# Output matmuls of one head alternate with score matmuls of a later head

## The chip, the cores and the metric

The kernel runs on one core of one Trainium2 chip. The metric is the device time in microseconds of one execution; the time before is the median of three runs. The engines are named as the profile does: PE is TensorE, with PEld for its weight loads (they overlap the matmuls), DVE is VectorE, ACT is ScalarE, POOL is GpSimd, and SP is the engine that issues most of the DMAs.

## The reference

Attention with two kinds of masks, and behind it a feed-forward layer on the attention's output. Batch 8, 8 heads, 576 positions, head size 64; heads 0 to 3 are local (each position sees the last 32), heads 4 to 7 strided (each position sees those at a distance of a multiple of 32). The feed-forward layer has 4608 tokens, 512 in, 2048 hidden.

```python
    pos = np.arange(S)
    rel = pos[:, None] - pos[None, :]
    mask_local = (rel >= 0) & (rel < stride)
    mask_strided = (rel >= 0) & (pos[None, :] % stride == pos[:, None] % stride)
...
    scores = np.where(masks[None, :, :, :], scores, -1000000000.0)
    scores = scores - np.max(scores, axis=-1, keepdims=True)
    attn = np.exp(scores)
    attn = attn / (np.sum(attn, axis=-1, keepdims=True) + 1e-09)
    return np.matmul(attn, v).astype(np.float32)
...
    h = np.maximum(x @ w_in, 0.0)
    return (h * h @ w_out).astype(np.float32)
```

## The kernel before

The tokens are cut into 12 chunks of 384. Each chunk has 16 slots of 128 hidden columns. For a slot, `up` (line 483) makes the hidden tile `h` from the chunk's `x` with 12 matmuls of 384 columns, ACT and DVE square it and split it into a high part `gh` and a low part `gl`, and `down` (line 512) adds it to the chunk's output `y` with 9 matmuls of 512 columns. Full precision comes from high and low halves: `x`, the weights, `q`, `k`, `v` and the probabilities are all split, the high half rounded by ACT (a cast), the low half the difference, mostly by POOL (`tensor_sub`).

While chunk c goes through the feed-forward layer, the attention for chunk c+1 is made. The strided heads are made on POOL, DVE and ACT alone (`strided`, line 414), and end with the tiles `xsh` (ACT) and `xsl` (POOL, line 476). The local heads need PE. For chunks 0 and 1 `pe_pair` makes them, two at a time. From chunk 2 on `pe_head` (line 208) makes one head in six steps, each a stretch of a Python generator up to its `yield`: load `qk` and `v`; cast (`kx` and `qx`, high halves on ACT, low halves on POOL in lines 229 and 231); score (four matmuls of 256 moving columns and 96 stationary ones, two to a bank, in line 248, with the mask added and the minimum taken by DVE); soft (exponentials and scaling on ACT); turn (`vx`, transposes on DVE, the probabilities split into `px` with a copy in a PSUM bank, lines 267 to 283); and output (four matmuls of 192 moving and 128 stationary columns, line 294, a copy by ACT and two additions by DVE to each bank of two). There are 40 such heads, four to a chunk.

PE's order is written out by hand. From slot 16 on the main loop (line 683) takes two slots at a time: two `up`, then two `down` of the slots before. The lists `plans` (line 603) say which heads go a step further: ahead of `up`, between `up` and `down`, and behind `down`. The first list is for chunk 1, the second for later chunks; they differ in where the first two heads are scored: between `up` and `down` in the first, ahead of `up` in the second. An instruction traced in `tc.issue_after(i)` stays behind `i` in the queue of `i`'s engine; it orders one engine only and is no wait. What isn't tied so is ordered by the compiler.

Three ties matter below. The last weight splits (POOL, line 180) are put behind `last["xs"]`, the strided `xsl` of chunk 1 (line 713). The steps for chunk 2's heads are put behind the last weight step of each engine (`weights_end`, line 615). And head 0 of chunk 2 is loaded and cast at slot 14 (line 724).

Of the kernel before, what the change touches and what calls it, by code (L numbers as in the profile page):

```python
# [7 lines left out]
F32 = mybir.dt.float32  # L8
# [79 lines left out]
def attn_moe(ctx: ExitStack, tc, qk_l, v_l, qk_d, v_d, qk_p, v_p, f_s, q_s, k_s, v_s, w_in, w_out, masks, eye, out):  # L88
# [117 lines left out]
    staged = {}  # L206

    def pe_head(c, h):
        u = f"{c}_{h}"

        def bank(nm):
            return psum(3 + next(turn) % 2, f"{nm}{u}")

        def buf(pl, nm, n, tag, **kw):
            return pl.tile([P, n], F32, name=f"{nm}{u}", tag=tag, **kw)

        qk, vp = buf(lraw, "qk", TC + KC, "qk"), buf(lraw, "v", NW * D, "v")
        qr, kr = qk[:, :TC], qk[:, TC:]
        vr = vp.rearrange("p (w d) -> p w d", d=D)
        kw, wins = KW, [(at, 0 if qc == 0 else 1) for _, qc, at in windows(c)]  # L220
        nk = wins[-1][0] + KW
        nc.sync.dma_start(out=qk[:, : TC + nk], in_=qk_l[c, h, :, : TC + nk])
        last["s"] = nc.sync.dma_start(out=vp, in_=v_l[c, h])
        yield

        qx = lpool.tile([P, TC], F32R, name=f"qx{u}", tag="qh", bufs=1)
        kx = lpool.tile([P, 2, KC], F32R, name=f"kx{u}", tag="kx", bufs=1)
        nc.scalar.copy(kx[:, 0, :nk], kr[:, :nk])
        nc.gpsimd.tensor_sub(kx[:, 1, :nk], kr[:, :nk], f32(kx[:, 0, :nk]))
        nc.scalar.copy(qx, qr)  # L230
        nc.gpsimd.tensor_sub(qx[D:], qr[D:], f32(qx[D:]))
        yield
        e = buf(lpool, "e", 512, "e")
        if h % 2 == 0:
            staged[c] = e
        nmax = small.tile([P, 2 * NW], F32, name=f"nm{u}", tag="nm")
        ssum = sums[h % 3]
        rs = small.tile([P, 2 * NW], F32, name=f"rs{u}", tag="rs")[:, :NW]
        cut = lambda w: slice(w * kw, (w + 1) * kw)
        reduce = lambda w, src, m: nc.vector.tensor_tensor_reduce(  # L240
            out=e[:QC, cut(w)], in0=src, in1=m, scale=-SCALE, scalar=3.0e38,
            op0=ALU.add, op1=ALU.min, accum_out=nmax[:QC, w : w + 1],
        )
        for a in range(0, NW, 2):
            s_ps = bank(f"s{a}")
            for w in (a, a + 1):
                k0 = wins[w][0]
                last["mm"] = nc.tensor.matmul(s_ps[:QC, 256 * (w - a) : 256 * (w - a + 1)], qx[:, w * QC : (w + 1) * QC], kx[:, :, k0 : k0 + kw], start=True, stop=True)  # L248
            sv = s_ps[:QC].rearrange("p (w t k) -> p w t k", w=2, t=2)
            m = wins[a][1]  # L250
            ev = e[:QC, a * kw : (a + 2) * kw].rearrange("p (w k) -> p w k", w=2)
            nc.vector.tensor_add(ev, sv[:, :, 1, :], mask_sb[:QC, m : m + 2, :])
            for w in (a, a + 1):
                reduce(w, sv[:, w - a, 0, :], e[:QC, cut(w)])
        yield
        for w in range(NW):
            nc.scalar.activation(e[:QC, cut(w)], e[:QC, cut(w)], AF.Exp, bias=nmax[:QC, w : w + 1], scale=-1.0, accum_out=ssum[:QC, w, :1])  # L257
        nc.vector.tensor_reduce(out=rs[:QC], in_=ssum[:QC, :NW], op=ALU.add, axis=AX.X)
        nc.vector.reciprocal(rs[:QC], rs[:QC])
        if h != HL - 1:  # L260
            for w in range(NW):
                nc.scalar.mul(e[:QC, cut(w)], e[:QC, cut(w)], rs[:QC, w : w + 1])  # L262
        else:
            ew = e[:QC, : NW * kw].rearrange("p (w k) -> p w k", k=kw)
            last["g"] = nc.gpsimd.tensor_mul(ew, ew, rs[:QC].unsqueeze(2).broadcast_to([QC, NW, kw]))
        yield
        vx = lpool.tile([P, NW, 2, D], F32R, name=f"vx{u}", tag="vx", bufs=1)
        nc.scalar.copy(vx[:, :, 0, :], vr)
        nc.gpsimd.tensor_sub(vx[:, :, 1, :], vr, f32(vx[:, :, 0, :]))
        pt = p_t[h % 2]  # L270
        for r in range(QC // STR):
            for k in (r, r + 1):
                nc.vector.transpose(  # L273
                    out=pt[STR * k : STR * (k + 1), :, STR * r : STR * (r + 1)],
                    in_=e.rearrange("p (w k) -> p w k", k=KW)[STR * r : STR * (r + 1), :, STR * k : STR * (k + 1)],
                )
        src = pt.rearrange("p w q -> p (w q)")
        px = lpool.tile([P, 2, TC], F32R, name=f"px{u}", tag="px")

        o_ps = bank("o0")  # L280
        nc.scalar.copy(o_ps[:, :TC], src)
        nc.scalar.copy(px[:, 0, :], src)
        nc.vector.tensor_sub(px[:, 1, :], o_ps[:, :TC], f32(px[:, 0, :]))
        yield
        x = x_tiles(c)
        par, hp = D * (h % 2), h // 2

        src = staged[c][par : par + D, :TC]
        for a in range(0, NW, 2):
            if a:  # L290
                o_ps = bank(f"o{a}")
            for w in (a, a + 1):
                sl = slice(w * QC, (w + 1) * QC)
                last["mm"] = nc.tensor.matmul(o_ps[:, 2 * QC * (w - a) : 2 * QC * (w - a + 1)], vx[:, w].rearrange("p t d -> p (t d)"), px[:, :, sl], start=True, stop=True)  # L294
            ov = o_ps[:, : 4 * QC].rearrange("p (w t q) -> p w t q", w=2, t=2)
            part = src[:, a * QC : (a + 2) * QC].rearrange("p (w q) -> p w q", w=2)
            nc.scalar.copy(part, ov[D:, :, 0, :])
            nc.vector.tensor_add(part, ov[:D, :, 1, :], part)
            nc.vector.tensor_add(part, ov[:D, :, 0, :], part)
        if par:  # L300
            src = staged[c][:, :TC]
            dst = [x["l", s][:, hp, :] for s in "hl"]
            last["a"] = nc.scalar.copy(dst[0], src)
            last["g"] = nc.gpsimd.tensor_sub(dst[1], src, f32(dst[0]))
        yield


    def pe_pair(c, pr, local, qk, vr, es, pt, banks, sm, single):
# [68 lines left out]
        p4 = pt.rearrange("p (h w q) -> p h w q", h=2, w=NW)  # L377
        for h in range(2):
            t = s_ps[h] if s_ps else banks()

            for w in [*range(NW)] * (2 if c == 0 and local and not pr and h else 1):
                nc.tensor.transpose(t[:kw, w * QC : (w + 1) * QC], e4[h][:, w], ident[:QC, :QC])
            if c == 0 and not local:
                nc.vector.tensor_copy(pt[:kw, h * TC : (h + 1) * TC], t[:kw, :TC])
            else:
                last["a"] = nc.scalar.copy(pt[:kw, h * TC : (h + 1) * TC], t[:kw, :TC])
        yield
        x = x_tiles(c)
        if local:
            o = s_ps[0] if s_ps else banks()  # L390

            for w in [*range(NW)] * (3 if c == 0 and not pr else 1):
                for h in range(2):
                    nc.tensor.matmul(o[D * h : D * (h + 1), w * QC : (w + 1) * QC], v4[:kw, h, w], p4[:kw, h, w], start=True, stop=True)
            outs = [(o[:, :TC], [x["l", s][:, pr, :] for s in "hl"])]
        else:
# [3 lines left out]
            for a in range(2):  # L400
                o = s_ps[a]
                for w in range(NW):
                    for h in range(2):
                        p0 = r0 + STR * h
                        nc.tensor.matmul(o[p0 : p0 + STR, w * QC : (w + 1) * QC], v4[:kw, h, w, STR * a : STR * (a + 1)], p4[:kw, h, w], start=True, stop=True)  # L405
# [163 lines left out]
    def pair_at(c, pr, local, place, psum_at):  # L569
        u = f"{c}_{pr}_{int(local)}"  # L570
        buf = lambda pl, nm, n, tag, **kw: pl.tile([P, n], F32, name=f"{nm}{u}", tag=tag, **kw)
        ee = lambda pl, tag: [buf(pl, f"e{h}", 512, tag) for h in range(2)]
        if place == 0:
            b = buf(lraw, "qk", TC + KC, "qk"), buf(lpool, "v", 512, "vx", bufs=1), ee(lpool, "e"), buf(lpool, "pt", 2 * TC, "px")
        elif place == 1:
            b = buf(lraw, "qk", TC + KC, "qk"), buf(ypool, "v", 512, "ysb"), ee(ypool, "ysb"), buf(lpool, "pt", 2 * TC, "px")
        elif place == 2:
            e = buf(xpool, "e", 2 * TC, "xlh")
            b = buf(xpool, "qk", 2 * TC, "xll"), buf(xpool, "v", 2 * TC, "xsl")[:, :512], [e[:, :TC], e[:, TC:]], buf(lpool, "pt", 2 * KC, "kx", bufs=1)[:, : 2 * TC]
        else:  # L580

            t = buf(wpool, "w", 2048, "w7")
            b = buf(xpool, "qk", 2 * TC, "xsh"), buf(spool, "v", 512, "s3", bufs=5), [t[:, :512], t[:, 512:1024]], t[:, 1024 : 1024 + 2 * TC]
# [10 lines left out]
    def local(c):  # L594
# [7 lines left out]
    heads = {}  # L602
    plans = (
        (("", "0", "01"), ("", "1", "012"), ("", "0", "123"), ("", "1", ""), ("2", "", "23"), ("3", "", "23"), ("", "2", "301"), ("", "3", "0")),
        (("0", "", "01"), ("1", "", "012"), ("", "0", "123"), ("", "1", ""), ("2", "", "23"), ("3", "", "23"), ("", "2", "301"), ("", "3", "0")),
    )

    def take(c, which):
# [213 lines left out]
```

## Time and profile before

| what | value |
| --- | --- |
| median of three runs | 873.07 us (872.31 to 874.12) |
| span of the profiled execution | 872.06 us (872.1 on the page) |
| instructions | 14656, of these 4773 matmuls |
| PE busy | 865.1 us |
| DVE, ACT, POOL busy | 640.3, 557.6, 650.6 us |
| mean granted clock of PE | 0.999 |
| output matmuls of `pe_head` (line 294) | 160, 23.4 us busy |
| score matmuls of `pe_head` (line 248) | 160, 25.4 us busy |

The profiled execution has no time of its own beside its span; the runs' median lies 1.0 us above the span. Busy times are unions, and matmuls overlap each other in the records (the end of one is modelled), so the pace of PE is read from the starts of its matmuls. "Granted clock" is the share of full speed that the chip allows PE: 1.00 is 2.4 GHz, 0.50 is 1.2 GHz.

### The profile page before, as it was taken

What the parts mean: (1) busy time and instruction counts of PE and PEld (TensorE: products, weight loads), DVE (VectorE), ACT (ScalarE), POOL (GpSimd) and SP (SyncE); (2) the same over time, 40 slices, a digit from 0 to 9 for tenths busy, and PEclk for the clock granted to TensorE, in tenths of its full rate; (3) what the DMA queues carried; (4) which work ended last, traced back from release to release, by engine and by line L of the source; (5) the groups of instructions that cost most, each with busy time, mean ns of one, the idle gap of its engine ahead of it and who ended that gap; (6) DMA issues with size and microseconds to landing.
All of it is one profiled execution on the core that took longest, in us unless ns stands there. A gap on an engine that the chain in (4) does not pass through costs nothing.

```text
span 872.1 us, 14656 instructions
## 1 busy us (share of the span) xinstructions
PE 865.1 (99%) x4773; PEld 788.0 (90%) x4773; DVE 640.3 (73%) x1902; ACT 557.6 (64%) x1479; POOL 650.6 (75%) x705
## 2 busy tenths in 40 slices
PE   8999999999999999999999999999999999999998
PEld 7888899999999999999999898999898989899997
DVE  5987688788787787877778778778788878762111
ACT  6989766667576576666666656747657566564332
POOL 3798878868887888788879978997998997850000
PEclk9999999999999999999999999999999999999999
DMA  9962521323123032113113202312212021000001
GB/s 354 365 233 82 184 84 46 95 82 109 40 76 104 26 112 84 38 68 104 39 32 98 80 13 75 104 32 75 77 53 80 14 71 61 8 1 1 37 1 37
DMA packets 26940, 71.39 MB, mean 82 GB/s; under 512 B 2992, under 2 KB 9008, under 8 KB 25328
## 3 DMA queue, kind: packets, MB, share of 16 engines
q1 hardware_dynamic: 26432, 70.00, 23.9%
q8 instruction: 37, 0.61, 0.3%
q10 hardware_dynamic: 432, 0.46, 0.2%
q14 instruction: 39, 0.32, 0.1%
HBM read 61.01 MB, written 9.44 MB: 81 GB/s over the span
## 4 chain that ended last, share of the span: by engine, by line
PE 93%; ACT 2%; POOL 2%; DVE 1%; issue 1%; DMA 1%; ACTq 0%; POOLq 0%
PE h L495 44%; PE y L532 44%; PE s L248 2%; PE o L294 2%; ACT b L366 1%; DMA raw<-w_out 1%; PE b L338 1%; POOL w L180 1%; PE w_ps L634 1%; PE b L405 0%; POOL pq L441 0%; DVE raw L170 0%; DVE sums L370 0%; ACT w L176 0%; ACT z L167 0%
## 5 line engine op out<-in xcount | busy, mean ns | idle before, releaser
L532 PE MATMUL y<-w,gh 128*128 128x512 f32 x1152 | 371.4, 391 | 0.4 <-ACT gh L507 0.4
L532 PEld LDWEIGHTS y<-w,gh 128*128 128x128 f32 x1152 | 215.9, 188 | 43.2 <-ACT gh L507 0.8
L464 POOL TENSOR_TENSOR pp<-vs,sc 128x448 f32<-128x448 f32 (+10 forms) x192 | 189.7, 1015 | 49.5 <-DVE qs L465 25.9
L495 PE MATMUL h<-xsh,w 128*128 128x384 f32 x768 | 226.2, 335 | 0.0
L532 PE MATMUL y<-w,gl 128*128 128x512 f32 x576 | 222.6, 390 | 0.0
L495 PE MATMUL h<-xlh,w 128*128 128x384 f32 x768 | 220.5, 337 | 0.0
L441 POOL TENSOR_TENSOR pq<-ks,qs 128x512 f32<-128x512 f32 (+2 forms) x192 | 197.8, 1050 | 24.6 <-DVE sc L442 23.0
L507 ACT CAST gh<-h 128x384 fp32r<-128x384 f32 x192 | 91.7, 477 | 105.0 <-PE y L532 102.7
L505 ACT ACTIVATE h<-h 128x384 f32<-128x384 f32 x176 | 82.6, 471 | 118.5 <-PE h L495 115.9
L508 DVE TENSOR_TENSOR gl<-h,gh 128x384 fp32r<-128x384 f32 x192 | 105.4, 549 | 69.0 <-ACT gh L507 68.0
L442 DVE TENSOR_REDUCE sc<-pq 128x8 f32<-128x512 f32 (+4 forms) x228 | 118.8, 534 | 48.3 <-POOL pq L441 45.3
L495 PEld LDWEIGHTS h<-xlh,w 128*128 128x128 f32 x768 | 140.4, 188 | 2.9
L495 PEld LDWEIGHTS h<-xsh,w 128*128 128x128 f32 x768 | 141.4, 188 | 0.5 <-POOL w L180 0.2
L495 PE MATMUL h<-xsl,w 128*128 128x384 f32 x384 | 128.4, 334 | 0.0
L465 DVE TENSOR_REDUCE qs<-pp 128x64 f32<-128x448 f32 (+11 forms) x192 | 107.2, 563 | 28.2 <-POOL pp L464 26.4
L495 PE MATMUL h<-xll,w 128*128 128x384 f32 x384 | 125.8, 336 | 0.0
L532 PEld LDWEIGHTS y<-w,gl 128*128 128x128 f32 x576 | 108.2, 188 | 19.4
L273 DVE STREAM_TRANSPOSE p_t<-e 32x128 f32<-32x128 f32 x240 | 72.4, 302 | 18.3 <-ACT e L262 13.0
L506 ACT ACTIVATE h<-h 128x384 f32<-128x384 f32 x176 | 82.9, 473 | 3.8
L257 ACT ACTIVATE e<-e,nm 96x128 f32<-96x128 f32 x160 | 62.5, 392 | 19.5 <-DVE nm L240 19.3
L495 PEld LDWEIGHTS h<-xll,w 128*128 128x128 f32 x384 | 71.8, 188 | 2.3
L495 PEld LDWEIGHTS h<-xsl,w 128*128 128x128 f32 x384 | 72.1, 188 | 0.1
(112 smaller groups left out, 1040.9 us busy)
## 6 DMA issues: line engine op xcount, KB each, us to landing
qk<-qk_l SPq DMA_DIRECT2D x24, 400.0 KB, 3.1
y<-ysb SPq DMA_DIRECT2D x35, 256.0 KB, 2.0
raw<-w_in SPq DMA_DIRECT2D x7, 1024.0 KB, 11.1
qk<-qk_l SPq DMA_DIRECT2D x16, 416.0 KB, 3.2
vs<-v_s SPq DMA_DIRECT2D x10, 576.0 KB, 3.8
raw<-w_out SPq DMA_DIRECT2D x5, 1024.0 KB, 12.9
v<-v_l SPq DMA_DIRECT2D x40, 128.0 KB, 2.1
ks<-k_s SPq DMA_DIRECT2D x8, 576.0 KB, 3.8
```

Of the source, the lines that this page charges most:

```text
L257: nc.scalar.activation(e[:QC, cut(w)], e[:QC, cut(w)], AF.Exp, bias=nmax[:QC, w : w + 1], scale=-1.0, accum_out=ssum[:QC, w, :1])
L273: nc.vector.transpose(out=pt[STR * k : STR * (k + 1), :, STR * r : STR * (r + 1)], in_=e.rearrange("p (w k) -> p w k", k=KW)[STR * r : STR ...
L441: nc.gpsimd.tensor_mul(pv, kt[:, a : a + m, :], qt[:, i - i0 : i - i0 + 1, :].broadcast_to([P, m, D]))
L442: nc.vector.tensor_reduce(out=sc[:, i - i0, a : a + m], in_=pv, op=ALU.add, axis=AX.X)
L464: nc.gpsimd.tensor_mul(pv, vt[:, a : a + nd, :n], sc[:, il : il + 1, :n].broadcast_to([P, nd, n]))
L465: nc.vector.tensor_reduce(out=ot[:, il, a : a + nd], in_=pv, op=ALU.add, axis=AX.X)
L495: done = nc.tensor.matmul(ph[:, :TC], wi[p][w][:, wsl], x["ls"[kt // 2], s][:, kt % 2, :], start=n == 0, stop=n == 11)
L505: nc.scalar.activation(g, g, AF.Relu)
L506: nc.scalar.activation(g, g, AF.Square)
L507: last["gh"] = nc.scalar.copy(gh, g)
L508: nc.vector.tensor_sub(gl, g, f32(gh))
L532: done = nc.tensor.matmul(into, g[:, t * P : (t + 1) * P], wo[p][w][:, wsl], start=j == fresh and k == 0, stop=j == NFT - 1 and k == 2)
```

## The change

`pe_head` becomes a class `Head` with the steps `load`, `cast`, `scores`, `soft`, `turn` and `outputs`. `scores(a)` and `outputs(a)` are now half heads: the two matmuls of one bank, returned as a list, and the work on that bank as a function. `visit(o, s)` takes half a head's outputs and half a head's scores of a later head, issues their matmuls in turn (output, score, output, score), each tied behind the one before, and then the work on both banks. All `visit`s stand on PE's queue where `plan` puts them: for each two slots g it gives steps ahead of `up`, two lists between `up` and `down`, and steps behind `down`. In the steady part (g from 14) there is one visit ahead of `up`, with the outputs of half v - 3 and the scores of half v, where v = g - 5; the first six g have their own lists. The outputs go to bank 4, the scores to bank 3.

Around it: outputs are gathered in a tile of their own (`st`) instead of the head's `e`; `px` has one buffer instead of two, `v` three instead of two; the probabilities of `pe_pair` are two tiles, one to each head, and its second place takes the buffers `st` and `qh`.

```diff
+    def chain(make):
+
+        with tc.issue_after(last["pe"].ins):
+            last["pe"] = make()
...
+        def scores(self, a, bank):
...
+            s = psum(bank, f"s{a}{self.u}")
+
+            def product(w):
+                q, k = self.qx[:, w * QC : (w + 1) * QC], self.kx[:, :, self.at[w] : self.at[w] + KW]
+                return nc.tensor.matmul(s[:QC, 256 * (w - a) : 256 * (w - a + 1)], q, k, start=True, stop=True)
...
+            return [lambda w=w: product(w) for w in (a, a + 1)], rest
...
+        def turn(self, bank):
+            self.vx = vx = lpool.tile([P, NW, 2, D], F32R, name=f"vx{self.u}", tag="vx", bufs=1)
...
+            self.px = px = lpool.tile([P, 2, TC], F32R, name=f"px{self.u}", tag="px", bufs=1)
+            copy = psum(bank, f"p{self.u}")[:, :TC]
+            nc.scalar.copy(copy, src)
+            nc.scalar.copy(px[:, 0, :], src)
+            nc.vector.tensor_sub(px[:, 1, :], copy, f32(px[:, 0, :]))
...
+    def visit(o=None, s=None, banks=(4, 3)):
+
+
+        jobs = [heads[n // 2].outputs(2 * (n % 2), banks[0]) for n in ([] if o is None else [o])]
+        jobs += [heads[n // 2].scores(2 * (n % 2), banks[1]) for n in ([] if s is None else [s])]
+        for two in zip(*(products for products, _ in jobs)):
+            for make in two:
+                chain(make)
+        behind_pe(*(rest for _, rest in jobs))
+
+    def behind_pe(*steps):
+        with tc.issue_after(last["pe"].ins):
+            for step in steps:
+                step()
...
-    plans = (
-        (("", "0", "01"), ("", "1", "012"), ("", "0", "123"), ("", "1", ""), ("2", "", "23"), ("3", "", "23"), ("", "2", "301"), ("", "3", "0")),
-        (("0", "", "01"), ("1", "", "012"), ("", "0", "123"), ("", "1", ""), ("2", "", "23"), ("3", "", "23"), ("", "2", "301"), ("", "3", "0")),
-    )
...
+    def plan(g):
+
+
+        n = len(heads)
+        head = lambda k, what: [(what, k)] if 0 <= k < n else []
+        t = g - 8
+        if t == 0:
+            return [("s", 0), ("S", 1)], [("cast", 1), ("soft", 0)], [], [("load", 2)]
+        if t == 1:
+            return [("s", 2), ("S", 3)], [("cast", 2), ("turn", 0)], [], [("soft", 1), ("load", 3)]
+        if t == 2:
+            return [("v", 0, 4)], [], [("v", 1, 5)], [("turn", 1), ("cast", 3), ("soft", 2)]
+        if t == 3:
+            return [("v", 2, None)], [], [("v", 3, None)], [("turn", 2), ("load", 4)]
+        if t == 4:
+            return [("s", 6), ("S", 7)], [("cast", 4), ("soft", 3)], [("v", 4, None)], [("load", 5)]
+        if t == 5:
+            return [("v", 5, 8)], [("turn", 3)], [], []
+        v = g - 5
+        k = v // 2
+        o = v - 3 if 0 <= v - 3 < 2 * n else None
+        s = v if v < 2 * n else None
+        visits = [("v", o, s)] if o is not None or s is not None else []
+        if v % 2:
+            return visits, head(k + 1, "cast") + head(k, "soft"), [], []
+        return visits, head(k - 1, "turn"), [], head(k + 1, "load")
+
+    def do(steps):
+        for what, *k in steps:
+            if what == "s":
+                visit(None, k[0])
+            elif what == "S":
+                visit(None, k[0], banks=(4, 4))
+            elif what == "v":
+                visit(*k)
+            else:
+                h = heads[k[0]]
+                step = getattr(h, what)
+                args = (4,) if what == "turn" else ()
                 with ExitStack() as st:
...
+                    for i in weights_end.values() if h.c == NPLAIN else ():
                         st.enter_context(tc.issue_after(i.ins))
...
+                    behind_pe(lambda: step(*args))
...
-            before, between, rest = plans[c >= NPLAIN][j // 2]
-            for part, slots, two in (up, (s, s + 1), before), (down, (s - 2, s - 1), between):
-                take(c + 1, two)
+            before, middle, between, rest = plan(s // 2)
+            for part, slots, then in (up, (s, s + 1), [before]), (down, (s - 2, s - 1), [middle, between]):
+                for steps in then:
+                    do(steps)
...
-            take(c + 1, rest.strip("01") if j >= NFT - 4 else rest)
-            if j >= NFT - 4:
-                take(c + 2, rest.strip("23"))
+            do(rest)
...
-            take(2, "010")
+            do([("load", 0), ("load", 1), ("cast", 0)])
```

## Rows read from the trace of the kernel before

**Rows 1.** The page's busy times by engine (share of the span, instructions), and its row of PE's granted clock in 40 slices of the span, in tenths.

```profile
PE 865.1 (99%) x4773; PEld 788.0 (90%) x4773; DVE 640.3 (73%) x1902; ACT 557.6 (64%) x1479; POOL 650.6 (75%) x705
...
PEclk9999999999999999999999999999999999999999
```

**Rows 2.** The page's chain of work that ended last, shares of the span by engine.

```profile
PE 93%; ACT 2%; POOL 2%; DVE 1%; issue 1%; DMA 1%; ACTq 0%; POOLq 0%
```

**Rows 3.** Who PE waited for, over the whole span: us in total, times, the longest. Six rows in all, of which the first two and the last are shown; the others are 0.5, 0.4 and 0.3 us.

```profile
PE w_ps L634 <- POOL sums L121: 1.6, 1, 1.6
PE b L382 <- DVE e L375: 0.5, 1, 0.5
...
PE b L382 <- POOL e L375: 0.2, 1, 0.2
```

**Rows 4.** Groups of PE's weight loads by line and shape, whole span: count, then busy us and the mean ns of one, then idle time ahead of them and what ended it.

```profile
L294 PEld LDWEIGHTS o<-px,vx 128*128 128x128 f32 x160 | 23.5, 189 | 0.0
L248 PEld LDWEIGHTS s<-kx,qx 128*96 128x96 f32 x160 | 22.2, 162 | 4.7 <-POOL qx L231 0.5
```

**Rows 5.** Timeline of PE around one visit of output matmuls (start us, duration us, instruction). The second and third line of the four output matmuls come from narrower windows, which leave out the first one and the first two of them.

```profile
303.65 0.34 PE L495 MATMUL h<-xsh,w 128*128 128x384 f32 x1
303.83 0.59 PE L294 MATMUL o<-px,vx 128*128 128x192 f32 x4
...
303.92 0.50 PE L294 MATMUL o<-px,vx 128*128 128x192 f32 x3
...
304.03 0.39 PE L294 MATMUL o<-px,vx 128*128 128x192 f32 x2
...
304.25 0.42 PE L532 MATMUL y<-w,gh 128*128 128x512 f32 x1
304.51 0.39 PE L532 MATMUL y<-w,gl 128*128 128x512 f32 x1
304.74 0.39 PE L532 MATMUL y<-w,gh 128*128 128x512 f32 x1
```

**Rows 6.** Timeline of PE around one visit of score matmuls, same columns.

```profile
413.12 0.40 PE L532 MATMUL y<-w,gh 128*128 128x512 f32 x1
413.36 0.63 PE L248 MATMUL s<-kx,qx 128*96 128x256 f32 x4
413.82 0.34 PE L495 MATMUL h<-xlh,w 128*128 128x384 f32 x1
414.00 0.34 PE L495 MATMUL h<-xll,w 128*128 128x384 f32 x1
```

**Rows 7.** Timeline of PE through the first two `up` of chunk 1 to the first scores and the `down` behind them.

```profile
97.94 1.55 PE L495 MATMUL h<-xlh,w 128*128 128x384 f32 x8
...
101.76 0.51 PE L495 MATMUL h<-xll,w 128*128 128x384 f32 x2
102.41 0.72 PE L248 MATMUL s<-kx,qx 128*96 128x256 f32 x4
102.97 0.39 PE L532 MATMUL y<-w,gh 128*128 128x512 f32 x1
```

**Rows 8.** The chain that ended last, in order of time, ahead of the first scores: start us, us, what.

```profile
97.87 1.02 POOL xsl L476
98.89 1.27 POOL w L180
100.16 1.12 POOL kx L229
...
101.35 1.02 POOL qx L231
```

**Rows 9.** The end: the last matmul in the timeline, then two stretches (from:to, length, busy us and instructions of PE, PEld, DVE, ACT and POOL, then PE's granted clock, the DMA share and GB/s).

```profile
868.43 0.28 PE L532 MATMUL y_rest<-w,gh 128*128 128x256 f32 x1
...
868.70:870.70 2.00, 0.01 (x1) 0.00 (x0) 0.42 (x1) 0.16 (x1) 0.00 (x0) 1.00 0.83 302
870.70:872.06 1.36, 0.00 (x0) 0.00 (x0) 0.00 (x0) 0.00 (x0) 0.00 (x0) 0.50 0.00 0
```

**Rows 10.** The start: three lines of PE's timeline, then the groups of line 338's matmuls in the stretches 1.5 to 7.1 and 7.3 to 9.1.

```profile
1.56 4.45 PE L634 MATMUL w_ps<-p_t 128*128 128x128 bf16 x40 [1.56 <-POOL sums L121]
5.94 3.23 PE L338 MATMUL b<-qk 64*96 64x128 f32 x48
9.11 3.24 PE L634 MATMUL w_ps<-p_t 128*128 128x128 bf16 x55
...
L338 PE MATMUL b<-qk 64*96 64x128 f32 x10 | 1.4, 433 | 0.0
...
L338 PE MATMUL b<-qk 64*96 64x128 f32 x22 | 1.4, 270 | 0.0
```

**Rows 11.** POOL's timeline behind the first scores: the last cast step of the second head.

```profile
107.31 1.01 POOL L231 TENSOR_TENSOR qx<-qk,qx 64x384 fp32r<-64x384 f32 x1
```

**Rows 12.** DVE's timeline behind the output visit of rows 5: the last two of its four additions.

```profile
306.59 0.62 DVE L299 TENSOR_TENSOR e<-o,e 64x192 f32<-64x192 f32 x2
```

**Rows 13.** Two lines of `turn`, over the whole span: durations in ns (least, median, most), first and last start, forms.

```profile
L281 ACT COPY o<-p_t x40: 452/479/492, 113.7 to 786.7; 128x384 f32<-128x384 f32 x40
...
L283 DVE TENSOR_TENSOR px<-o,px x40: 514/545/560, 114.2 to 787.2; 128x384 fp32r<-128x384 f32 x40
```

**Rows 14.** POOL's timeline ahead of the first casts; in brackets the idle time ahead of an instruction and what ended it.

```profile
97.87 1.02 POOL L476 TENSOR_TENSOR xsl<-qkvs,xsh 128x384 fp32r<-128x384 f32 x1 [0.78 <-ACT xsh L475]
```

More of the change, by code (lines that the diff above doesn't have):

```diff
@@ L203, in x_tiles @@
         return xt[c]
[L206 to L242, printed above, removed]
-        )
[L244 to L260, printed above, removed]
-            for w in range(NW):
[L262 to L305, printed above, removed]
@@ new lines, in chain, with __init__, buf, load @@
+    def chain(make):
+        with tc.issue_after(last["pe"].ins):
+            last["pe"] = make()
+    outs = {}
+    class Head:
+        def __init__(self, n):
+            self.n = n
+            self.c, self.h = NPLAIN + n // HL, n % HL
+            self.u = f"{self.c}_{self.h}"
+            self.first = [1 - (qc == 0) for _, qc, _ in windows(self.c)]
+            self.at = [at for _, _, at in windows(self.c)]
+        def buf(self, pl, nm, n, tag, **kw):
+            return pl.tile([P, n], F32, name=f"{nm}{self.u}", tag=tag, **kw)
+        def load(self):
+            c, h = self.c, self.h
+            qk, vp = self.buf(lraw, "qk", TC + KC, "qk"), self.buf(lraw, "v", NW * D, "v", bufs=3)
+            self.qr, self.kr = qk[:, :TC], qk[:, TC:]
+            self.vr = vp.rearrange("p (w d) -> p w d", d=D)
+            self.nk = self.at[-1] + KW
+            nc.sync.dma_start(out=qk[:, : TC + self.nk], in_=qk_l[c, h, :, : TC + self.nk])
+            last["s"] = nc.sync.dma_start(out=vp, in_=v_l[c, h])
+        def cast(self):
+            nk = self.nk
+            self.qx = qx = lpool.tile([P, TC], F32R, name=f"qx{self.u}", tag="qh", bufs=1)
+            self.kx = kx = lpool.tile([P, 2, KC], F32R, name=f"kx{self.u}", tag="kx", bufs=1)
+            nc.scalar.copy(kx[:, 0, :nk], self.kr[:, :nk])
+            nc.gpsimd.tensor_sub(kx[:, 1, :nk], self.kr[:, :nk], f32(kx[:, 0, :nk]))
+            nc.scalar.copy(qx, self.qr)
+            nc.gpsimd.tensor_sub(qx[D:], self.qr[D:], f32(qx[D:]))
+        def scores(self, a, bank):
+            if a == 0:
+                self.e = self.buf(lpool, "e", 512, "e")
+                self.nmax = small.tile([P, NW], F32, name=f"nm{self.u}", tag="nm")
+            s = psum(bank, f"s{a}{self.u}")
+            def product(w):
+                q, k = self.qx[:, w * QC : (w + 1) * QC], self.kx[:, :, self.at[w] : self.at[w] + KW]
+                return nc.tensor.matmul(s[:QC, 256 * (w - a) : 256 * (w - a + 1)], q, k, start=True, stop=True)
+            def rest():
+                sv = s[:QC].rearrange("p (w t k) -> p w t k", w=2, t=2)
+                ev = self.e[:QC].rearrange("p (w k) -> p w k", k=KW)
+                m = self.first[a]
+                nc.vector.tensor_add(ev[:, a : a + 2], sv[:, :, 1, :], mask_sb[:QC, m : m + 2, :])
+                for w in (a, a + 1):
+                    nc.vector.tensor_tensor_reduce(
+                        out=ev[:, w], in0=sv[:, w - a, 0, :], in1=ev[:, w], scale=-SCALE, scalar=3.0e38,
+                        op0=ALU.add, op1=ALU.min, accum_out=self.nmax[:QC, w : w + 1],
+                    )
+            return [lambda w=w: product(w) for w in (a, a + 1)], rest
+        def soft(self):
+            ev = self.e[:QC].rearrange("p (w k) -> p w k", k=KW)
+            ssum = sums[self.n % 3]
+            rs = small.tile([P, NW], F32, name=f"rs{self.u}", tag="rs")
+            for w in range(NW):
+                nc.scalar.activation(ev[:, w], ev[:, w], AF.Exp, bias=self.nmax[:QC, w : w + 1], scale=-1.0, accum_out=ssum[:QC, w, :1])
+            nc.vector.tensor_reduce(out=rs[:QC], in_=ssum[:QC, :NW], op=ALU.add, axis=AX.X)
+            nc.vector.reciprocal(rs[:QC], rs[:QC])
+            if self.h != HL - 1:
+                for w in range(NW):
+                    nc.scalar.mul(ev[:, w], ev[:, w], rs[:QC, w : w + 1])
+            else:
+                last["g"] = nc.gpsimd.tensor_mul(ev, ev, rs[:QC].unsqueeze(2).broadcast_to([QC, NW, KW]))
+        def turn(self, bank):
+            self.vx = vx = lpool.tile([P, NW, 2, D], F32R, name=f"vx{self.u}", tag="vx", bufs=1)
+            nc.scalar.copy(vx[:, :, 0, :], self.vr)
+            nc.gpsimd.tensor_sub(vx[:, :, 1, :], self.vr, f32(vx[:, :, 0, :]))
+            pt = p_t[self.h % 2]
+            for r in range(QC // STR):
+                for k in (r, r + 1):
+                    nc.vector.transpose(
+                        out=pt[STR * k : STR * (k + 1), :, STR * r : STR * (r + 1)],
+                        in_=self.e.rearrange("p (w k) -> p w k", k=KW)[STR * r : STR * (r + 1), :, STR * k : STR * (k + 1)],
+                    )
+            src = pt.rearrange("p w q -> p (w q)")
+            self.px = px = lpool.tile([P, 2, TC], F32R, name=f"px{self.u}", tag="px", bufs=1)
[3 more added lines that the diff above has]
+            nc.vector.tensor_sub(px[:, 1, :], copy, f32(px[:, 0, :]))
+        def outputs(self, a, bank):
+            par, hp = D * (self.h % 2), self.h // 2
+            if a == 0 and not par:
+                outs[self.c, hp] = self.buf(lpool, "st", TC, "st", bufs=1)
+            o = psum(bank, f"o{a}{self.u}")
+            def product(w):
+                v, p = self.vx[:, w].rearrange("p t d -> p (t d)"), self.px[:, :, w * QC : (w + 1) * QC]
+                return nc.tensor.matmul(o[:, 2 * QC * (w - a) : 2 * QC * (w - a + 1)], v, p, start=True, stop=True)
+            def rest():
+                x = x_tiles(self.c)
+                st = outs[self.c, hp]
+                ov = o[:, : 4 * QC].rearrange("p (w t q) -> p w t q", w=2, t=2)
+                part = st[par : par + D, a * QC : (a + 2) * QC].rearrange("p (w q) -> p w q", w=2)
+                nc.scalar.copy(part, ov[D:, :, 0, :])
+                nc.vector.tensor_add(part, ov[:D, :, 1, :], part)
+                nc.vector.tensor_add(part, ov[:D, :, 0, :], part)
+                if par and a:
+                    dst = [x["l", s][:, hp, :] for s in "hl"]
+                    last["a"] = nc.scalar.copy(dst[0], st)
+                    last["g"] = nc.gpsimd.tensor_sub(dst[1], st, f32(dst[0]))
+            return [lambda w=w: product(w) for w in (a, a + 1)], rest
@@ new lines, in attn_moe @@
+    heads = [Head(n) for n in range(HL * (NCHUNK - NPLAIN))]
+    def visit(o=None, s=None, banks=(4, 3)):
[9 more added lines that the diff above has]
+                step()
@@ L598, in local @@
             yield
-    heads = {}
-    plans = (
-        (("", "0", "01"), ("", "1", "012"), ("", "0", "123"), ("", "1", ""), ("2", "", "23"), ("3", "", "23"), ("", "2", "301"), ("", "3", "0")),
-        (("0", "", "01"), ("1", "", "012"), ("", "0", "123"), ("", "1", ""), ("2", "", "23"), ("3", "", "23"), ("", "2", "301"), ("", "3", "0")),
-    )
-    def take(c, which):
-        if NPLAIN <= c < NCHUNK:
-            for h in map(int, which):
-                if (c, h) not in heads:
-                    heads[c, h] = pe_head(c, h)
+    def plan(g):
[22 more added lines that the diff above has]
+        return visits, head(k - 1, "turn"), [], head(k + 1, "load")
@@ L616, in take @@
                         st.enter_context(tc.issue_after(i.ins))
-                    last.pop("mm", None)
-                    next(heads[c, h])
-                    last["pe"] = last.get("mm", last["pe"])
+                    behind_pe(lambda: step(*args))
     ungated = convert()
```

21 lines of the change are left out of this document (11 added, 10 removed).

## The prediction

> **What bounds the kernel now.** I read the page's busy shares first. PE is busy for 865.1 of 872.1 us, and the other engines sit at 64 to 75% [rows 1]. The chain that ended last gives PE 93% of the span and every other engine 2% or less [rows 2]. In the list of who waited for whom, PE has six waits, all named, and 3.4 us together [rows 3]; the list misses one stall of 0.3 us, which comes below. So nothing that ACT, DVE, POOL or the DMA queues lose or gain counts, unless PE comes to wait for it. PE's own time is then read from the starts of its matmuls, not from their durations (0.33 to 0.34 us for 384 columns [rows 5]), since they overlap. In the timeline the `h` matmuls start 0.17 to 0.18 us apart and the `y` matmuls of 512 columns 0.23 apart [rows 5, 6]: some 2.2 columns per ns, without a gap.
>
> **The gain: two kinds of matmul alternate.** A visit of output matmuls has four of them with 192 moving columns. At the rate of the `h` matmuls (24 from 97.94 on, the last two from 101.76 [rows 7]: 3.82 for 22, 0.174 us for 384 columns) one needs 0.087 us. They start at 303.83, 303.92, 304.03, the `y` behind them starts at 304.25, and the next `y` 0.26 after it instead of 0.23 [rows 5]. So four cost 0.42 + 0.03 = 0.45 us where the columns need 0.35. The weight loads explain it: a load of 128 columns takes 189 ns and one of 96 columns 162, and loads behind short matmuls follow each other at 0.11 us, which is longer than 0.087 [rows 4, 5]. Four score matmuls take 413.36 to 413.82, 0.117 us each, as 256 columns should [rows 6]; their 96-column loads are 27 ns shorter, so by the spacing of 0.112 one needs about 0.085 us. Put an output matmul ahead of each score matmul and both loads are covered: the 96-column load (0.085) by the output matmul (0.087), the 128-column load (0.112) by the score matmul (0.117). A pair then costs 0.204 us instead of 0.112 + 0.117 = 0.229, a gain of 0.025.
>
> From the plan, 74 visits hold a half head of each kind (two at t = 2, one at t = 5, then v = 9 to 79), two pairs each: 148 x 0.025 = 3.8 us. The six output visits and six score half-heads that stay alone keep their price. Against it, entries: `y` to score costs 0.24 instead of 0.23 [rows 6], output behind `h` 0.18 instead of 0.17 [rows 5], and the first `h` behind the scores takes 0.18 [rows 6]; a head now has two visits between `y` and `h` instead of one of each kind, some 8 ns more for 37 heads' worth, 0.3 us. The gain is 3.5 us. Its bounds: if every change between the two kinds cost the 6 ns of the change from `y` to score, 296 changes take 1.8 us of it; if the loads don't overlap, it is nothing; the upper end is 3.8.
>
> **The price: the first scores move ahead of the first chunk's `up`.** In the old plan for chunk 1 (the first of the two lists) head 0 of chunk 2 is scored between `up` and `down` of the slot pair at g = 8. The new `plan` at t = 0 puts ("s", 0), ("S", 1) in the part done before `up`. Each matmul is chained behind the one before, so `up(1, 0)` can't pass them. In the trace that `up` starts at 97.94, and the score only at 102.41, behind both slots of `up` [rows 7]. It waits there already: two `h` start from 101.76 on, at 0.174 each the score would be due at 102.11, and it comes 0.30 later. What it waits for stands in the chain, in order of time: POOL does the strided `xsl` (97.87), the last weight split (98.89), the low half of `kx` (100.16), the low half of `qx` (101.35 to 102.37), then comes the score [rows 8]. That order is tied: the last splits are put behind `xs`, and the casts of chunk 2 behind the last weight step. Nothing in the diff touches these. So the score is ready at 102.41 again, and PE stands from 97.94: 102.41 - 97.94 = 4.47, less the 0.30 that is in the trace now, 4.17 us more. The cover that is gone is 24 `h` matmuls. PE has no idle time later that could absorb it [rows 3]. The bounds are 0 (if POOL's steps came 4.4 us earlier) and 4.47. I take 4.17.
>
> **What the stall does to the clock.** At the end of the trace the last matmul starts at 868.43 and takes 0.28; the granted clock is 1.00 to 870.70 and 0.50 from there on [rows 9]. So it fell to 1.2 GHz some 2 us after the last matmul, though PE had been dense until then. A stall of over 4 us is twice that. The way back shows at the start: 40 equal matmuls take 4.45 us, 0.111 each, and 55 of the same form 3.24, 0.059 each; in between the first ten of the next form last 433 ns, and later ones 270 [rows 10]. From 1.56 on the engine ran at the lower level for some 5.5 us of work (the 4.45 and those first ten), which lost half of that, 2.8 us. After the stall the loss lies between 0 (the clock holds, or is back as PE resumes) and 2.8 (as from the start). I take 1.9, nearer the row of the start, and less because the engine was at full rate just before.
> The Trainium skill, "TensorE: Matmul & The Clock Gate", Part 1 (The HAM clock gate), says that the throttled level is the default and that activity releases it, so that an idle stretch costs half speed afterwards. The trace agrees (1.00 to 0.50 at 870.70); by that rule the 1.9 is due, and without it the sum is 1.9 lower.
>
> **Smaller parts.** The instructions of ACT, DVE and POOL are the same in number and form; DMA loads too. In the steady part a cast follows its predecessor's scores and has a whole slot pair, 24 x 0.174 + 18 x 0.23 = 8.3 us, until the next visit; now, behind scores that end at 102.97, POOL's two `tensor_sub` end at 108.3 [rows 11]: 5.4 us. `turn` has as long; no cost. In two places it is shorter. At t = 2 and 3 the outputs of head 0 stand ahead of a `down`, and the next PE step that needs `turn` (outputs of head 1, then scores in bank 4) stands right behind that `down`, 18 `y` matmuls or 4.1 us later. `turn` needs the bank that the outputs leave: at 304.25 an output visit has ended, its last DVE step ends at 307.21, 3.0 us later [rows 12], and the copy to the bank (0.48) and the subtraction (0.55) come behind [rows 13]: 4.0 us. A half visit leaves less to do, so I take 0.2 us for both, bounds 0 and 1.5. The split `pt` tiles and the third `v` buffer: nothing, PE doesn't wait for either now.
>
> **Sum.** 872.06 (span) - 3.5 + 4.17 + 1.9 + 0.2 = 874.8. The median of the runs, 873.07, lies 1.0 above the span of the profiled execution, so the forecast is 875.8 us.
>
> **Rivals.**
> 1. *The stall comes, the clock holds.* For it: PEclk is 9 in all forty slices [rows 1]. Against it: the fall at 870.70. Time: 875.8 - 1.9 = 873.9.
> 2. *No stall, faster.* One mechanism: POOL finishes `qx` of head 0 about 4.4 us earlier, since the compiler orders the casts ahead of the `xsl` and split steps. It decides below a first score at about 100.7: then the stall is under 3 us, the clock's price is small and the 3.5 us of gain outweigh both. For it: the scheduler is free to order what isn't tied, and POOL sat idle for 0.78 us ahead of `xsl` [rows 14]. Against it: the ties named above. Time: 873.07 - 3.5 + 0.2 = 869.8.
> 3. *The alternation does not do what it says.* The 96-column load isn't hidden by an 87 ns matmul, or the change between kinds costs what it saves. For it: load (0.085) and matmul (0.087) are equal to 2 ns. Against it: the durations differ by the columns, as they should. Time: 875.8 + 3.5 = 879.3 at most, 877.5 if half of the gain is left.
>
> **How the numbers follow.** Forecast 0.55, rival 1 0.16, rival 2 0.16, rival 3 0.08; the remaining 0.05 are waits of PE for `turn` or casts beyond the 0.2. About 0.2% of this kernel (1.75 us) can be told from no change: faster is below 871.3, slower above 874.8. The forecast with its own range (gain 1.7 to 3.8, clock 1.2 to 2.8) runs from 874.3 to 878; some 0.07 of its chance lies below 874.8. Slower: 0.48 + 0.08 + 0.05, some 0.61. Same: rival 1 and that part of the forecast, 0.23. Faster: rival 2, 0.16. The range of 8 in 10 goes from 869.6, which takes in most of rival 2, to 877.6, which leaves out the worst of rival 3.
>
> **What would show it.** Right: one wait of PE at some 98 us, of over 4 us, for POOL's `qx`; a granted clock below 1 in the stretch from there to about 108; in the steady part visits where output and score matmuls alternate, four of them in 0.41 us, and a chunk of eight slot pairs that is 8 x 0.05 = 0.4 us shorter. Wrong: no wait at 98, or four alternating matmuls in 0.46 us, or waits of PE that come back in every chunk.

## The result, and the profile after

The changed kernel takes 877.98 us (median of four runs, 877.96 to 878.68) where the kernel before takes 873.10; the ratio is 1.0058, 95% interval 1.0044 to 1.0073. It is slower, as forecast, but by 4.9 us and not 2.7, and 0.4 us beyond the range. The profiled execution spans 876.0 us and took 877.98, 2.0 us more; the forecast had set 1.0 between the span before and the median of other runs. That changes no term of the sum, but spans of single executions differ by their start (PE's first `up` comes 1.0 us earlier in this profile than in the one before), so stages are compared below.

The page looks the same: PE 99% busy, and the clock row all nines.

```profile
PE 863.5 (99%) x4773; PEld 785.7 (90%) x4773; DVE 645.3 (74%) x1902; ACT 562.7 (64%) x1479; POOL 651.9 (74%) x705
...
PE 90%; POOL 3%; DVE 3%; ACT 2%; issue 1%; DMA 0%; POOLq 0%; ACTq 0%; DVEq 0%
```

Beside [rows 1] PE's busy time fell by 1.6 us, though the kernel is slower; beside [rows 2] PE lost 3% of the chain to POOL and DVE. What the chain names, the list of who PE waited for shows near its top (us in total, times, the longest):

```profile
PE s L251 <- POOL qx L241: 4.2, 1, 4.2
...
PE o L306 <- ACT e L271: 1.1, 1, 1.1
PE o L306 <- DVE px L296: 0.7, 1, 0.7
```

Beside [rows 3] three waits are new: one of 4.2 us for `qx` and two of about 1 us ahead of output matmuls. The first stands where [rows 7] had `up`. In PE's timeline (start us, us, instruction) the `y` matmuls of slot 13 end, and the scores come 4.6 us after the start of the last one:

```profile
95.70 0.85 PE L565 MATMUL y<-w,gh 128*128 128x512 f32 x3
100.76 1.17 PE L251 MATMUL s<-kx,qx 128*96 128x256 f32 x4 [4.20 <-POOL qx L241]
101.72 1.48 PE L528 MATMUL h<-xlh,w 128*128 128x384 f32 x4
```

and the chain, in order of time, has POOL's four steps of [rows 8] ahead of them, in the same order and as long:

```profile
96.30 1.00 POOL xsl L509
97.30 1.25 POOL w L180
98.55 1.09 POOL kx L239
...
99.71 1.00 POOL qx L241
```

The four score matmuls fill 0.97 us instead of the 0.47 of [rows 6]: they run at half the clock. The stretches around them (length, busy us of PE, PEld, DVE, ACT, POOL, then the granted clock, the DMA share, GB/s) give it:

```profile
88.00:96.10 8.10, 8.10 (x42) 7.15 (x41) 6.85 (x17) 7.45 (x16) 6.66 (x8) 1.00 0.46 155
96.20:100.50 4.30, 0.35 (x2) 0.00 (x0) 1.33 (x3) 0.89 (x3) 4.12 (x4) 1.00 0.74 224
100.60:103.90 3.30, 3.14 (x11) 3.15 (x12) 2.02 (x13) 1.81 (x7) 3.16 (x10) 0.50 0.86 303
104.00:108.00 4.00, 4.00 (x23) 3.83 (x22) 1.98 (x8) 3.14 (x11) 3.45 (x4) 1.00 0.36 106
```

It is 1.00 while PE stands still, 0.50 from just before PE resumes until 103.9, and 1.00 again. The stretch from the start of the last `y` of slot 13 to that of slot 15 has the same matmuls in both kernels. It runs from 97.71 to 106.86 in the kernel before (the first two lines here, third matmul of each) and from 96.16 to 110.80 in the changed one (the line at 95.70 above and the last one here):

```profile
97.25 0.85 PE L532 MATMUL y<-w,gh 128*128 128x512 f32 x3
...
106.41 0.84 PE L532 MATMUL y<-w,gh 128*128 128x512 f32 x3
...
110.35 0.85 PE L565 MATMUL y<-w,gh 128*128 128x512 f32 x3
```

That is 9.15 us before and 14.65 after: 5.5 us for the stall and the clock.

The two other waits, in PE's timeline: the second half of head 0's outputs, behind the `up` of t = 2, and the first half of head 1's, behind the `down` of t = 2 (ahead of the `up` of t = 3).

```profile
124.26 0.34 PE L528 MATMUL h<-xsh,w 128*128 128x384 f32 x1
125.65 0.33 PE L306 MATMUL o<-px,vx 128*128 128x192 f32 x1 [1.05 <-ACT e L271]
...
130.02 0.39 PE L565 MATMUL y<-w,gh 128*128 128x512 f32 x1
131.15 0.44 PE L306 MATMUL o<-px,vx 128*128 128x192 f32 x2 [0.74 <-DVE px L296]
```

The first comes 1.39 us behind an `h` that lasts 0.174, the second 1.13 behind a `y` that lasts 0.227: 1.2 + 0.9 = 2.1 us. The releaser of the first (an exponential on ACT) has nothing to do with an output; the bank that it needs is bank 4, which the first half's outputs filled one `up` earlier, and it is left by the second of DVE's two additions, from 125.16 to 125.50. ACT's copy of that bank was done at 120.90. DVE's timeline has these steps, among others, ahead of the additions (lines 314 and 315):

```profile
119.67 1.87 DVE L287 STREAM_TRANSPOSE p_t<-e 32x128 f32<-32x128 f32 x6
...
123.09 0.41 DVE L257 TENSOR_TENSOR e<-s,mask_sb 96x256 f32<-96x256 f32 x1
123.43 0.54 DVE L541 TENSOR_TENSOR gl<-h,gh 128x384 fp32r<-128x384 f32 x1
123.89 0.34 DVE L314 TENSOR_TENSOR st<-o,st 64x192 f32<-64x192 f32 x1
...
125.16 0.34 DVE L315 TENSOR_TENSOR st<-o,st 64x192 f32<-64x192 f32 x1
```

In the steady part the visits alternate as planned, and the chunks are shorter. First a visit, then the first `h` of chunk 7 and of chunk 8 in the changed kernel:

```profile
253.72 0.25 PE L306 MATMUL o<-px,vx 128*128 128x192 f32 x1
253.81 0.28 PE L251 MATMUL s<-kx,qx 128*96 128x256 f32 x1
253.93 0.25 PE L306 MATMUL o<-px,vx 128*128 128x192 f32 x1
254.01 0.28 PE L251 MATMUL s<-kx,qx 128*96 128x256 f32 x1
254.13 0.34 PE L528 MATMUL h<-xlh,w 128*128 128x384 f32 x1
...
524.20 0.34 PE L528 MATMUL h<-xlh,w 128*128 128x384 f32 x1
...
593.85 0.34 PE L528 MATMUL h<-xlh,w 128*128 128x384 f32 x1
```

and the same two in the kernel before:

```profile
518.74 0.34 PE L495 MATMUL h<-xlh,w 128*128 128x384 f32 x1
...
588.66 0.34 PE L495 MATMUL h<-xlh,w 128*128 128x384 f32 x1
```

A visit takes 0.417 us here (0.425 in some, 0.418 on average), an output 0.09 and 0.08, a score 0.12. A chunk takes 69.65 us instead of 69.92: 0.27 less, 0.033 to each of eight visits, 2.5 us for 74.

So 5.5 (stall and clock) + 2.1 (two waits) - 2.5 = 5.1; measured are 4.9. That they agree to 0.2 us is partly luck. From the last `y` of slot 13 to the last matmul the two profiles differ by 5.5 us (770.7 before, 776.2 after), so 0.4 us of that part stand in none of the three terms. Between the first `up` and slot 13, which the change hardly touches, the changed kernel's profile is 0.5 us shorter; the kernel before has one wait of 0.4 us there (`y` for `gh`) that the changed one lacks. Why is open.

### The profile page after: what moved, and what is told of

The parts are those of the page before. It is cut to its first block, busy times and chain, and to the rows that moved or that the text cites. A ratio compares the mean times of both kernels' runs of the same rounds, so it can differ in the third digit from the quotient of the medians.

```text
span 876.0 us, 14661 instructions
## 1 busy us (share of the span) xinstructions
PE 863.5 (99%) x4773; PEld 785.7 (90%) x4773; DVE 645.3 (74%) x1902; ACT 562.7 (64%) x1479; POOL 651.9 (74%) x705
## 4 chain that ended last, share of the span: by engine, by line
PE 90%; POOL 3%; DVE 3%; ACT 2%; issue 1%; DMA 0%; POOLq 0%; ACTq 0%; DVEq 0%
PE h L528 43%; PE y L565 42%; PE s L251 2%; PE o L306 2%; POOL w L180 1%; ACT b L399 1%; POOL pp L497 1%; POOL pq L474 1%; PE b L371 1%; DMA raw<-w_out 0%; PE w_ps L693 0%; DVE gl L541 0%; PE b L438 0%; DVE raw L170 0%; DVE sc L475 0%
```

## The experiments

**First the stall: is it the place of the first scores?** In `a1_first_later` the scores of head 0 go behind the two `up`, in `a2_both_later` those of head 1 too.

```diff
-            return [("s", 0), ("S", 1)], [("cast", 1), ("soft", 0)], [], [("load", 2)]
+            return [], [("s", 0), ("S", 1), ("cast", 1), ("soft", 0)], [], [("load", 2)]
...
-            return [("s", 2), ("S", 3)], [("cast", 2), ("turn", 0)], [], [("soft", 1), ("load", 3)]
+            return [], [("s", 2), ("S", 3), ("cast", 2), ("turn", 0)], [], [("soft", 1), ("load", 3)]
```

> The four score matmuls of head 0 (t = 0) go behind the two up of chunk 1, where the kernel before has them. Theory (the stall of PE for qx at 96 us and the half clock behind it cost 4.1 + 1.4 us): both go, PE waits 0.3 us for qx as before, and since the scores of head 1 stay ahead of the next up, 18 y matmuls or 4.1 us later, their casts (5.5 us behind the first scores in the kernel before) come up to 1.4 us late: 872.5 to 874.0 us. Rival (PE has to wait for POOL there wherever the scores stand, the wait only moves): no change, 878.0 us.

> The scores of head 0 and of head 1 (t = 0 and 1) both go behind the up, as in the kernel before. Theory: the stall and the half clock go, and no wait of more than 0.3 us is left at the first two heads; the two waits at t = 2 and 3 (1.1 and 0.7 us in the list) stay: 872.4 us. Rival (the wait only moves): 878.0 us. A second rival (the early scores shift the later steps, and the waits at t = 2 and 3 are a consequence of the stall): they go as well, 870.4 us.

Measured: 873.86 us with the first edit (ratio to the kernel before 1.0013, 1.0003 to 1.0022) and 872.73 with both (1.0000, 0.9990 to 1.0009), ten runs each. The wait doesn't move along: `up` fills the time as it did before, and 5.25 us come back with both edits; the first rival falls. With the first alone, the scores of head 1 come too early for their cast, as expected (PE's timeline of `a1_first_later`):

```profile
107.28 0.60 PE L251 MATMUL s<-kx,qx 128*96 128x256 f32 x3 [1.16 <-POOL qx L241]
```

In `a2_both_later` the clock stays up in that stretch. The two waits at t = 2 and 3 remain (1.1 and 0.5 us in its list), so they don't follow from the stall; the second rival falls.

**How much of it is the clock?** `b1_fill` gives PE something to do in the stall; the results are read by nothing.

```diff
+            if s == NFT:
+                fill = psum(3, "fill")
+                unit = ident[:, : P // 2].bitcast(BF16)
+                with tc.issue_after(last["pe"].ins):
+                    for _ in range(70):
+                        last["mm"] = nc.tensor.matmul(fill[:, :P], unit, unit, start=True, stop=True)
+                last["pe"] = last["mm"]
```

> 70 idle matmuls of 128 columns (into bank 3, read by nothing) stand on PE ahead of the first scores, some 3.9 us at 0.056 us each, so that PE works while it waits for qx. Theory (part of the loss is the clock, which falls because PE stands still): the granted clock stays at 1.00, the scores start when they did, and 1.4 us come back: 876.6 us. Rival (the clock does not follow from the stall, or costs nothing): 878.0 us, with the clock still at 0.50 for 3.4 us. The stall itself stays either way.

PE's timeline and the stretch behind the stall in `b1_fill`:

```profile
95.95 4.08 PE L760 MATMUL fill<-ident 128*128 128x128 bf16 x70
100.22 0.71 PE L251 MATMUL s<-kx,qx 128*96 128x256 f32 x4 [0.19 <-POOL qx L241]
100.77 0.87 PE L528 MATMUL h<-xlh,w 128*128 128x384 f32 x4
...
100.60:103.90 3.30, 3.30 (x21) 3.30 (x20) 2.27 (x13) 2.37 (x9) 3.22 (x10) 1.00 0.86 317
```

The clock is 1.00, 21 matmuls run in the 3.3 us in which 11 ran, and the scores take 0.55 us instead of 0.97. The stretch from the last `y` of slot 13 to that of slot 15 takes 13.14 us instead of 14.65: the clock cost 1.5 us, the stall 4.0. The time is 877.04 us (four runs, 875.92 to 877.62), 0.94 less; the four runs are too far apart to tell this from 1.5, which is the trace's figure.

**Is it the alternation that gains?** In `c1_in_turn_off` a visit issues both outputs and then both scores.

```diff
-        for two in zip(*(products for products, _ in jobs)):
-            for make in two:
+        for products, _ in jobs:
+            for make in products:
                 chain(make)
```

> In a visit both output matmuls come first and then both score matmuls; nothing else changes. Theory (the second output matmul waits for its 128-column weight load, 0.112 instead of 0.087 us, and nothing else differs): a visit takes some 0.437 instead of 0.417 to 0.425 us, 74 visits cost 0.9 to 1.5 us: 879.2 us. Rival (the gain of the steady part comes from fewer changes between up and down or from the merged visits, not from alternating): 878.0 us, and visits of the same length as now.

Measured: 879.03 us, 1.05 more than the changed kernel, and no run of the one reaches into the range of the other. A visit and the first `h` of chunk 7 and chunk 8 in its timeline:

```profile
254.53 0.36 PE L306 MATMUL o<-px,vx 128*128 128x192 f32 x2
254.72 0.40 PE L251 MATMUL s<-kx,qx 128*96 128x256 f32 x2
254.96 0.34 PE L528 MATMUL h<-xlh,w 128*128 128x384 f32 x1
...
525.32 0.51 PE L528 MATMUL h<-xlh,w 128*128 128x384 f32 x2
...
595.08 0.51 PE L528 MATMUL h<-xlh,w 128*128 128x384 f32 x2
```

The visit takes 0.43 us, two outputs 0.2 of it, and this chunk 69.76 us: 0.11 more than with alternation, and still 0.16 less than before. Other chunks differ by less: from the first `h` of chunk 2 to that of chunk 10, with 64 visits, the timelines have 559.71 us before, 557.51 with alternation and 558.15 without, so 0.64 us for the order and 2.20 in all. For 74 visits that makes 0.7 of 2.5 us for the order within a visit; what else of the 1.05 us in the run times is the order's was not told apart. The other 1.8 come with the joint visits, and with what they change beside `up` and `down`. The starts of the weight loads, 0.109 to 0.112 us apart where they follow each other, would explain that: of four outputs in a row the loads of the third, the fourth and the `y` behind them come late (these matmuls start 0.111 to 0.114 us behind the one ahead, instead of 0.088); of two outputs that scores follow, only the load of the first score does. No run took these loads apart.

**The two waits: queue order or too much work?** All three kernels stand on `a2_both_later`. `e3_act_tie` puts head 2's exponentials behind the copy of head 1's `turn` on ACT; `e2_dve_tie` puts a visit's score work behind its output additions on DVE, and the transposes of head 1 behind the last addition of head 0's first half; `e1_both_ties` has both.

```diff
+            last["copied"] = nc.scalar.copy(copy, src)
...
+                    if what == "soft" and k[0] == 2:
+                        st.enter_context(tc.issue_after(last["copied"].ins))
...
+                last["added"] = last["added", 2 * self.n + a // 2] = nc.vector.tensor_add(part, ov[:D, :, 0, :], part)
...
+        behind_pe(jobs[0][1])
+        for _, rest in jobs[1:]:
+            with tc.issue_after(last["added"].ins):
+                behind_pe(rest)
...
+                if self.n == 1:
+                    st.enter_context(tc.issue_after(last["added", 0].ins))
```

> The kernel of a2_both_later, with the DVE ties of e2_dve_tie and the ACT tie of e3_act_tie together. Theory (each of the two waits at t = 2 and 3 is a queue order, DVE's for the first and ACT's for the second): both fall to under 0.3 us, 872.7 - 2.0 = 870.7 us, and the kernel is faster than the one before by some 0.25%. Rival (there is too much work for 4.1 us, whatever its order): the waits keep 1.5 us or more in sum, 872.4 us.

> On a2_both_later: on DVE the mask and minimum steps of a visit's scores stand behind its output additions, and the transposes of head 1 behind the last addition of head 0's first half. Theory: the first wait (PE for the bank of head 0's first half, 1.1 us) goes, the second (for px of head 1, 0.5 us and 0.2 around it) stays: 872.7 - 1.2 = 871.5 us. Rival (the first wait has another cause than the additions' place in DVE's queue): 872.7 us.

> On a2_both_later: on ACT the exponentials and scalings of head 2 (soft) stand behind the copy to the bank in head 1's turn. Theory: that copy comes some 1.1 us earlier, and the second wait (0.5 us and 0.2 around it) goes, the first stays: 872.7 - 0.7 = 872.0 us. Rival (the copy waits for DVE's additions and not for ACT's queue): 872.7 us, with the second wait as it was.

Measured: `e3_act_tie` 872.01 us (ten runs; ratio to before 0.9988, 0.9979 to 0.9997), as its theory said; the second wait is gone from its list, and the first is there with 1.1 us. `e2_dve_tie` 873.70 (ten runs) and `e1_both_ties` 873.97 (eleven): both slower than without the DVE ties, against the theory. The waits of `e2_dve_tie` at the two places, and DVE's timeline ahead of the first:

```profile
PE s L251 <- DVE nm L259: 1.4, 1, 1.4
...
PE o L309 <- DVE rs L272: 0.5, 1, 0.5
...
117.23 0.35 DVE L317 TENSOR_TENSOR st<-o,st 64x192 f32<-64x192 f32 x1
117.62 0.35 DVE L318 TENSOR_TENSOR st<-o,st 64x192 f32<-64x192 f32 x1
117.89 0.41 DVE L257 TENSOR_TENSOR e<-s,mask_sb 96x256 f32<-96x256 f32 x1
118.22 0.47 DVE L504 TENSOR_REDUCE qkvs<-pp 128x64 f32<-128x320 f32 x1
118.62 1.87 DVE L290 STREAM_TRANSPOSE p_t<-e 32x128 f32<-32x128 f32 x6
120.52 0.29 DVE L259 CUSTOM_DVE_ANT_0 e<-s,e 96x128 f32<-96x128 f32 x1
```

The additions end at 117.97, in time. But the transposes (1.87 us) now stand ahead of the minima of the scores, which leave bank 3, and the next half's scores need that bank. PE waits for the other bank instead, and for longer (1.4 us instead of 1.1). In `e1_both_ties` the list has the same 1.4 us, and 0.5 us for `px`: with the DVE ties the ACT tie no longer removes the second wait. In PE's waits that is some 0.3 us more than in `a2_both_later` and 0.8 more than in `e3_act_tie`, where the run times are 1.0 and 2.0 longer; the rest was not told apart. So `f1_transposes_later` ties the transposes alone, on `e3_act_tie`:

> On e3_act_tie: on DVE the transposes of head 1 (1.9 us) stand behind the last addition of head 0's first half; nothing else is tied (e2_dve_tie also put the minima of the scores behind the additions, and the transposes ahead of the minima). Theory (the first wait is those transposes' place ahead of the additions): the additions end 1.2 us or more earlier, ahead of the visit that needs the bank, the wait of 1.1 us goes and no other comes for it: 872.0 - 1.2 = 870.8 us. Rival (DVE has more than 4.1 us of work there, and whichever step stands last keeps PE waiting, as in e2_dve_tie): 872.0 us or more, with a wait of 1 us under another name.

Measured: 871.49 us (eleven runs; ratio to before 0.9987, 0.9978 to 0.9997), 0.5 less than `e3_act_tie` and not 1.2; the two intervals overlap, so the times alone don't tell these two apart. Its list has no wait for the bank of the first half any more, but the second is back, 0.8 us for `px` of head 1:

```profile
PE o L309 <- DVE px L299: 0.8, 1, 0.8
```

Both theories hold in part: each wait is the place of one step in a queue, and can be moved out of PE's way, but with 4.1 to 4.2 us between one `visit` and the next the step behind it comes late in turn. This version is faster than both kernels, by 1.4 us than the one before (0.3 to 1.9 by the interval): the 2.5 us of gain less some 1.0 of wait that is left (1.21 us from the `y` ahead of it instead of 0.23). That all waits could go at once was not shown.

## Why the prediction was wrong

- The stall. Right in place, releaser and order of POOL's steps; 4.17 us were forecast, and the stretch without the clock's share shows 4.0.
- The clock. Right that it falls, with 1.5 us instead of 1.9 and until 103.9 instead of about 108. It came back 3.2 us after PE resumed, sooner than the 5.5 us of work at the start [rows 10], so the row of the start was the wrong neighbour.
- The gain. Right that it comes, sized at 3.5 us and measured at 2.5. (148 x 0.025 is 3.7 and not 3.8, so the working gives 3.4.) Most of the miss is the 0.117 us of a score: next to an output it takes 0.121 to 0.125, so that a visit needs 0.417 to 0.425 us and not 0.408, 0.7 us for 74 visits. The fixed 8 ns for entries didn't hold it. The other 0.3 us lie in `up` and `down`: by the averages of the two timelines, the two `up` and two `down` of one head are 11 ns shorter than before, where the forecast has 22 (the 0.03 us behind the outputs less the 8 ns). The slower pace of `y` behind `h` (last section) is part of that: outputs between `up` and `down` had spared half of these places before.
- The two short places at t = 2 and 3. This is the step that failed: "I take 0.2 us for both, bounds 0 and 1.5", and the two waits measured 2.1 us, the largest miss of the sum. The step looked for places where `turn` has only a `down` to finish in, and named two: from head 0's second outputs to head 1's first, and from head 1's second to the scores in bank 4. The first of these is the second wait, 0.9 us; its 4.0 us of 4.1 were worked out, and then cut because "a half visit leaves less to do". At the other no wait came. The first wait, 1.2 us, stands at a place that the prediction had no term for: at t = 2 both halves of head 0's outputs use bank 4, one `up` of 4.2 us apart. There the copy and the two additions of the first half have to be done, and by the 3.0 us of [rows 12] they would fit. But the first half's visit ends at 120.23, and its additions start at 123.89 and 125.16, since DVE has transposes, two `gl`, a mask step and work of the strided heads ahead of them. Chains that fit at the durations of their own steps (3.0 of 4.2 us, 4.0 of 4.1) did not fit behind what else stood in the queues of two shared engines.
- The range. Its upper end was 877.6. With either the waits or the gain as forecast (1.9 and 1.0 us off) the time would have been inside. And the forecast's own range was added up wrongly: with a gain of 1.7 to 3.8 and a clock of 1.2 to 2.8 its terms give 874.8 to 878.5 and not 874.3 to 878, so none of its chance lay below 874.8, and 877.98 lies inside its upper end.
- Rivals. The clock holds: fell. No stall: fell; the ties held POOL's order. No gain from alternation: fell as it was put, since the steady part gains 2.5 us; `c1_in_turn_off` shows that the order gives the smaller part of it. The 877.5 us that this rival gives for half of the gain are near the measured time by luck. The remainder ("waits of PE for `turn` or casts beyond the 0.2"), held at 0.05, is what came for 0.9 us; the other 1.2 us were a wait for the outputs' own bank, for which the prediction had no rival.

With the measured terms in place of the forecast ones, 873.1 + 4.0 + 1.5 + 2.1 - 2.5 = 878.2 us, against 877.98; the 0.4 and 0.5 us that the sum leaves out (above) nearly cancel.

## What to carry to other kernels

When a step moves ahead of work on the engine that bounds a kernel, look up when its input is ready in the trace; a wait of 0.3 us there can be the visible end of one that 4 us of other work cover. Where a bank or a buffer has to turn round within a time that the sum of its steps nearly fills, count the steps that stand ahead of it in each shared queue, or expect a wait (0.9 and 1.2 us here). Short matmuls can gain from a neighbour of another shape: the later outputs of a row started 0.111 us apart here, and an output ahead of a score took 0.085 to 0.088. But most of what is gained here (1.8 of 2.5 us) comes from having fewer outputs in a row.

## What was not expected of the hardware

A matmul's pace depends on what stands beside it. In a row of four scores each starts the next 0.116 to 0.118 us later, and the last of them the `h` 0.116 later (averages of the kernel before); in the alternating visits of the changed kernel, where an output stands ahead of each score, the next output or `h` starts 0.121 to 0.125 us later. And `y` matmuls directly behind `h` are slower at first than behind outputs. In the changed kernel, behind an `h`, the first and the eleventh `y`:

```profile
258.30 0.39 PE L565 MATMUL y<-w,gh 128*128 128x512 f32 x1
...
260.61 0.39 PE L565 MATMUL y<-w,gl 128*128 128x512 f32 x1
```

Ten intervals take 2.31 us, 0.231 each. Behind outputs in the kernel before, the eleventh `y` counted from the second one (304.51 in [rows 5]):

```profile
306.77 0.62 PE L532 MATMUL y<-w,gh 128*128 128x512 f32 x2
```

Ten intervals take 2.26 us, 0.226 each. The cause of neither was tried.
